# Spectral filter and MLP, two layers: the first quad's layer norm in the output stage, the middle's staging buffers, and three smaller placements

## The chip, the cores and the metric

The kernel runs on one NeuronCore of a Trainium2 chip. The metric is the device time of one execution, in microseconds. The engines that matter are TensorE (PE, matmuls; its weight loads are shown as PEld), VectorE (DVE), ScalarE (ACT), GpSimd (POOL) and SyncE (SP, here an issuer of DMAs). Each engine runs its own instructions in order, and they wait for each other through semaphores.

## The reference

An array x of 2048 rows (sequence) and 576 columns goes twice through a spectral layer and an MLP, each with a residual:

```
def _A_ref(x, w_r, w_i):                       # spectral
    X = rfft2(x); X = X * (w_r + 1j * w_i)
    return irfft2(X, s=(S, D))
def _B_ref(x, w1, b1, w2, b2):                 # MLP
    y = _layernorm(x)
    h = gelu(y @ w1 + b1)                      # 576 -> 4608
    return h @ w2 + b2                         # 4608 -> 576
x = x + _A_ref(_layernorm(x)); x = x + _B_ref(_layernorm(x))     # and once more
```

Inputs and the result are bf16.

## The kernel before

The 2048 rows stand in SBUF as 16 tiles of 128 rows (`x_sb`), and the tiles are worked in the order `order`, four quads of four tiles. The Fourier transforms are matmuls with constant matrices. Each of the two layers has these stages.

- **First transform** (`SpectralIn`): along the columns, then the first step along the rows, with an exchange through DMAs into `vx`. In layer 1 nearly all of it is done inside the MLP of layer 0.
- **Middle** (`middle`, L610): for each of 16 groups n, `dft_u` transforms on TensorE into a two-bank accumulator (`big_ps`, of which there are three) and ScalarE copies it to a staging buffer `xs` (L623). `weigh` multiplies it on VectorE with the filter's real and imaginary part (L632, L633), `join` adds or subtracts the products (L639, L641), `idft_c` (L654) transforms back into another of the three accumulators, ScalarE copies the result to `h` (L662), and a DMA exchanges it into `hx` (L602). The loop issues `dft_u(i)`, then `idft_c(i-4)`, then `weigh(i)`. The `xs` buffers are three, two in `shared` and one in `h_sb`.
- **Output stage** (`SpectralOut`, L682): `idft_v(n)` (L696) transforms rows into a small accumulator (`sm_ps`, one bank, of which there are two), ScalarE copies it to `u2` (L703). `idft_v_rest(q)` (L728) does the last 34 rows for four tiles at once and is copied to `u2r` (L733). `idft_k(n)` (L753) transforms along the columns into a two-bank accumulator, and `add(n)` puts the result on x with VectorE (L773 for both halves, then L781 and L782, which `add(n+1)` issues as the odd part of tile n). Four tiles (`early`) have x put into the accumulator by TensorE and take a copy on ScalarE (L765) and two adds (L767).
- **Layer norm of the first quad**, by `Prep`, inside the output stage: sums and squares on ScalarE (L833), the moments on VectorE (L842 to L844), the root on ScalarE (L848), reciprocal and shift on VectorE (L853, L854), then a norm for each of four tiles, on VectorE (L875) or ScalarE (L862), each with a copy of the last 64 columns (L878 on VectorE, L865 on GpSimd), and `turn` (L895): five transposes on TensorE into a small accumulator and a copy to `yT` (L897). `pieces[n]` and `behind_add[n]` in `run_all` (L784) say behind which tile each of these is issued.
- **MLP**: `mlp_up` (L919, L927, gelu L933) for a quad of four tiles, then `mlp_down` (L966) for each tile, 72 matmuls into one two-bank accumulator and one add (L989). The last tile of a layer runs its two column halves one after the other (L971 to L982); in the last layer each half has its own accumulator and is stored with its own DMA.

The program's order on TensorE, VectorE, ScalarE and GpSimd is the order in which the code issues it (`manual_schedule`, L240). SP's order is the scheduler's: it puts each DMA where its waits allow. A wait belongs to a whole tile: a tile is one buffer or accumulator, and a writer waits for its readers even where they use other parts of it. An accumulator that is asked for goes to the buffer that is free first, and its first writer waits for the last reader of what stood there.

Of the kernel before, what the change touches and what calls it, by code (L numbers as in the profile page):

```python
# [161 lines left out]
def kernel(  # L162
# [447 lines left out]
    def middle(vx, hx, wks, i1s, loads, ahead, steps):  # L610
        st = {}
        r_sb = shared_tile(BF16)

        def dft_u(n):
            e = E_ORDER[n]
            for call in steps.get(n, ()):
                call()
            px = ahead.px[n] if n in steps else big_ps([P, 2, 512])
            for o, terms in ((0, ((0, 0), (1, 1))), (1, ((0, 1), (2, 0)))) if n not in steps else ():
                for q, (pl, ri) in enumerate(terms):  # L620
                    nc.tensor.matmul(px[:, o, 0:KP], lhsT=c_f2[:, n // 4, pl, n % 4, :], rhs=vx[:, E_SLOTS.index(e), ri, :], start=(q == 0), stop=(q == 1))  # L621
            xs = at(r_sb, [P, 2, KP], 592 * (n % 3)) if n % 3 < 2 else at(h_sb, [P, 2, KP], 4 * GROUP + 2 * 592 + 1024)
            nc.scalar.copy(out=xs[:], in_=px[:, :, 0:KP])  # L623
            st["xs", n] = xs

        def weigh(n):
            wk = wks[n // 4]
            xs = st.pop(("xs", n))
            ma, mb = (at(r_sb, [P, 2, KP], 592 * (2 + 4 * b + n % 4)) for b in (0, 1))
            wr = wk[:, n % 4, 0:1, 0:KP].to_broadcast([P, 2, KP])  # L630
            wi = wk[:, n % 4, 1:2, 0:KP].to_broadcast([P, 2, KP])
            nc.vector.tensor_mul(out=ma[:], in0=xs[:], in1=wr)  # L632
            nc.vector.tensor_mul(out=mb[:], in0=xs[:], in1=wi)  # L633
            st["m", n] = ma, mb

        def join(n):
            ma, mb = st.pop(("m", n))
            xp = at(r_sb, [P, 2, KP], 592 * (2 + 8 + n % 3))
            marks["xp", n] = nc.vector.tensor_sub(out=xp[:, 0, :], in0=ma[:, 0, :], in1=mb[:, 1, :]).ins  # L639
            if n not in SUMS_ON_PE:  # L640
                marks["xp", n] = nc.vector.tensor_tensor(out=xp[:, 1, :], in0=ma[:, 1, :], in1=mb[:, 0, :], op=ALU.add).ins  # L641
            for call in loads.get(n, ()):
                call(("xp", n))
            st["xp", n] = xp[:, 0], (ma[:, 1], mb[:, 0]) if n in SUMS_ON_PE else (xp[:, 1],)

        def idft_c(n):
            re, im = st.pop(("xp", n))
            i1 = i1s[n // 4]
            ph = big_ps([P, 2, 512])
            odd = big_ps([P, 2, 512]) if n == NT - 1 else ph  # L650
            for o, (p_re, p_im) in enumerate(((0, 2), (1, 0))):
                terms = [(p_re, re)] + [(p_im, part) for part in im]
                for q, (pl, rhs) in enumerate(terms):
                    nc.tensor.matmul(  # L654
                        (ph, odd)[o][:, o, 0:KP], lhsT=i1[:, pl, n % 4, :], rhs=rhs, start=(q == 0), stop=(q == len(terms) - 1)
                    )
            h = at(r_sb, [P, 2, KP], 592 * (13 + n % 8)) if n % 8 < 6 else at(h_sb, [P, 2, KP], 4 * GROUP + 592 * (n % 8 - 6))
            if n == NT - 1:
                nc.scalar.copy(out=h[:, 0], in_=ph[:, 0, 0:KP])
                ins = nc.vector.tensor_copy(out=h[:, 1], in_=odd[:, 1, 0:KP]).ins  # L660
            else:
                ins = nc.scalar.copy(out=h[:], in_=ph[:, :, 0:KP]).ins  # L662
            marks["h", n] = ins
            exchange(hx, E_ORDER[n], h, nc.gpsimd if n < NT - 3 else nc.sync, N_FIRST if n == NT - 1 else 0)
            st["h"] = h

        for i in range(NT + 4):
            if i < NT:
                dft_u(i)
            if 0 <= i - 4 < NT:  # L670
                idft_c(i - 4)
            if NT < i < NT + 3:
                keep_busy(1)
            if i < NT:
                weigh(i)
            for n in (i,) if i < 3 else range(max(3, i - 1), min(i, NT)):
                join(n)
        return st["h"]
# [3 lines left out]
    class SpectralOut:  # L682
# [33 lines left out]

        def idft_v_rest(self, q):

            pr = sm_ps([P, 4, P], F32)
            for i in range(4):  # L720
                for part, p0 in ((0, 0), (1, 64)):
                    cs = slice(part * 128, part * 128 + 128)
                    n = 4 * q + i
                    terms = [(self.hx[:, n, ri], c_r1[:, ri, cs]) for ri in range(2)]
                    if n < N_FIRST:
                        terms += [(self.late_h[:, ri], r1_late[:, n, ri, cs]) for ri in range(2)]
                    for k, (rows, rhs) in enumerate(terms):
                        nc.tensor.matmul(  # L728
                            pr[p0 : p0 + 64, i, :], lhsT=rows[:, KP - 64 : KP], rhs=rhs, start=(k == 0), stop=(k == len(terms) - 1)
                        )  # L730
            u2r = u2r_buf[u2r_turn[0] % 2]
            u2r_turn[0] += 1
            nc.scalar.copy(out=u2r[:], in_=pr[:])  # L733
            self.st["u2r", q] = u2r
# [49 lines left out]
        def run_all(self, prep, loads):  # L784

            pieces = {n: [] for n in range(NT)}
            for n, (i, k) in zip((1, 2, 3, 4, 5, 5, 6, 7), ((i, k) for i in range(4) for k in range(2))):
                pieces[n].append(lambda i=i, k=k: prep.sum(i, k))
            pieces[10].append(prep.root)
            for i, m in enumerate((13, 14, 14)):  # L790
                pieces[m].append(lambda i=i: prep.turn(i, "act"))
            behind_add = {9: [prep.moments], 11: [prep.scale_sums, lambda: prep.norm(0, nc.vector)], 12: [lambda: prep.norm(2, nc.vector)]}
            pieces[12].append(lambda: prep.norm_act(1))
            pieces[13].append(lambda: prep.norm_act(3))
            for n in self.early[:2]:
                self.put_x(n)
            for n in range(N_FIRST):
                self.idft_v_late(n)
            keep_busy(7, big_ps)
            self.idft_v(0)  # L800
            for call in loads:
                tc.add_manual_dep(call(), marks["u2", 0].name, SYNC, reason="pace of the loads")
            self.idft_v(1)
            self.idft_v_rest(0)
            self.idft_v(2)
            for n in range(NT):
                if n == NT - 1:
                    prep.turn(3, "act")
                if n in self.early[2:]:
                    self.put_x(n)  # L810
                self.idft_k(n)
                self.add(n)
                for call in behind_add.get(n, ()):
                    call()
                if 0 < n < NT - 2:
                    self.idft_v(n + 2)
                if n % 4 == 1 and n + 3 < NT:
                    self.idft_v_rest(n // 4 + 1)
                for call in pieces[n]:
                    call()  # L820
            self.add(NT)

    class Prep:
# [35 lines left out]
        def norm_act(self, i):  # L859
            rs, shift = self.rs_shift  # L860
            xn = work.tile([P, 640], BF16, tag="xn", bufs=3)
            nc.scalar.activation(  # L862
                out=xn[:, 0:D], in_=x_sb[:, self.quad[i], :], func=ACT.Identity, bias=shift[:, i : i + 1], scale=rs[:, i : i + 1]
            )
            nc.gpsimd.tensor_copy(out=xn[:, D:640], in_=xn[:, D - 64 : D])  # L865
            self.st[i] = xn
# [90 lines left out]
    def mlp_down(t, i, hts, store, between):  # L957
# [2 lines left out]
        xr = x_sb[:, t, :].rearrange("p (h n) -> p h n", h=2)  # L960
        nc.vector.tensor_tensor(out=xb[:], in0=xr, in1=b2_bc[:].rearrange("p (h n) -> p h n", h=2), op=ALU.add)  # L961
        po = big_ps([P, 2, 512])
        parts = [po, big_ps([P, 2, 512]) if t == order[-1] and store else po]

        def step(fc, h):
            nc.tensor.matmul(  # L966
                parts[h][:, h, 0:DH], lhsT=hts[fc][:, i * 128 : (i + 1) * 128], rhs=w2_chunk(fc)[:, h * DH : (h + 1) * DH],
                start=(fc == 0), stop=(fc == NFC - 1),
            )

        if t == order[-1]:  # L971
            for n in range(2 * NFC):
                h, fc = divmod(n, NFC)
                step(fc, h)
                if fc == NFC - 1:
                    nc.vector.tensor_tensor(out=xr[:, h], in0=parts[h][:, h, 0:DH], in1=xb[:, h], op=ALU.add)
                    if store:
                        nc.sync.dma_start(out=ov[:, t, h * DH : (h + 1) * DH], in_=xr[:, h])
                if n % 12 == 11:
# [13 lines left out]
    def mlp(li, prep, spec, loads):  # L993
# [3 lines left out]
        for q in range(4):  # L997
# [6 lines left out]
                spec.ahead = Ahead(spec.vx, spec.st)  # L1004
            for i, t in enumerate(QUADS[q]):
                if q == 3 and spec is not None and i == 2:
                    for out, in_ in ((spec.ahead.w[96:128], late_ap), (c_k1_late[:], k1_late_ap[1])):
                        ins = nc.sync.dma_start(out=out, in_=in_).ins
                        tc.add_manual_dep(ins, marks["ht", NFC - 1].name, SYNC, reason="pace of the loads")
                slots = {k: [] for k in range(6)}  # L1010
                if q < 3 and i == 0:
                    slots[0].append(prep.stats)
# [135 lines left out]
```

## Time and profile before

| | us |
|---|---|
| median of three runs (730.92, 732.32, 732.39) | 732.32 |
| the profiled execution | 730.92 |
| its span | 729.2 |

TensorE's granted clock is 1.0 throughout. Busy time and number of instructions by stage, from the windows of the profile (us from the span's start):

| stretch | what | PE | DVE | ACT | POOL |
|---|---|---|---|---|---|
| 32.0 to 58.9 | layer 0, end of the first transform and middle | 25.44 | 20.83 | 18.73 | 7.77 |
| 58.9 to 85.0 | layer 0, output stage | 24.74 | 19.90 | 21.69 | 1.95 |
| 85.0 to 387.0 | layer 0, MLP, with layer 1's first transform | 301.62 | 113.74 | 111.71 | 27.81 |
| 387.0 to 414.4 | layer 1, end of the first transform and middle | 26.70 | 19.52 | 19.68 | 14.43 |
| 414.4 to 440.4 | layer 1, output stage | 24.57 | 19.77 | 21.56 | 0.48 |
| 440.4 to 729.2 | layer 1, MLP and the last store | 285.40 | 46.21 | 88.93 | 13.45 |

How to read it: TensorE is busy nearly all the time. In the MLPs the other engines have more than half of the time to spare; in the middle and the output stage, two times 27 and 26 us, all three compute engines are busy for three quarters of the time or more. A line of the timeline gives the start, the time from the first start to the last end, engine, source line, operation, what is written from what, and in brackets the idle time before it with what ended it. A line of the chain gives start, length and what was on the path.

### The profile page before, as it was taken

What the parts mean: (1) busy time and instruction counts of PE and PEld (TensorE: products, weight loads), DVE (VectorE), ACT (ScalarE), POOL (GpSimd) and SP (SyncE); (2) the same over time, 40 slices, a digit from 0 to 9 for tenths busy, and PEclk for the clock granted to TensorE, in tenths of its full rate; (3) what the DMA queues carried; (4) which work ended last, traced back from release to release, by engine and by line L of the source; (5) the groups of instructions that cost most, each with busy time, mean ns of one, the idle gap of its engine ahead of it and who ended that gap; (6) DMA issues with size and microseconds to landing.
All of it is one profiled execution on the core that took longest, in us unless ns stands there. A gap on an engine that the chain in (4) does not pass through costs nothing.

```text
span 729.2 us, 12472 instructions
## 1 busy us (share of the span) xinstructions
PE 718.1 (98%) x5078; PEld 456.9 (63%) x5078; DVE 267.0 (37%) x917; ACT 309.5 (42%) x534; POOL 79.5 (11%) x139
## 2 busy tenths in 40 slices
PE   8999999999999999999999999999999999999998
PEld 5777645864587448744877674477447744774476
DVE  7894910664055504520367586011400140110011
ACT  7796764026411651156216686610550056005600
POOL 4240112002000200000006301200100010000000
PEclk9999999999999999999999999999999999999999
DMA  9788345211111111100217402530102010200000
GB/s 291 215 194 202 141 150 194 66 44 54 37 39 50 55 32 41 47 7 1 59 40 235 134 2 71 188 115 18 44 1 45 17 45 1 45 19 8 1 17 17
DMA packets 52722, 54.33 MB, mean 75 GB/s; under 512 B 31576, under 2 KB 43624, under 8 KB 52664
## 3 DMA queue, kind: packets, MB, share of 16 engines
q1 hardware_dynamic: 43784, 25.99, 13.5%
q0 software_dynamic: 8448, 26.96, 11.7%
q8 instruction: 40, 0.66, 0.4%
q10 hardware_dynamic: 432, 0.58, 0.2%
q14 instruction: 18, 0.15, 0.1%
HBM read 29.31 MB, written 8.59 MB: 52 GB/s over the span
## 4 chain that ended last, share of the span: by engine, by line
PE 95%; ACT 2%; DVE 1%; DMA 1%; issue 0%; SPq 0%; POOL 0%; ACTq 0%; POOLq 0%
PE psb_4486 L966 1%; PE psb_6902 L966 1%; PE psb_6304 L966 1%; PE psb_5706 L966 1%; PE psb_4228 L966 1%; PE psb_4100 L966 1%; PE psb_3294 L966 1%; PE psb_2492 L966 1%; PE psb_2126 L966 1%; PE psb_1998 L966 1%; PE psb_7654 L966 1%; PE psb_7577 L966 1%; PE psb_7500 L966 1%; PE psb_7185 L966 1%; PE psb_7108 L966 1%; PE psb_6587 L966 1%
## 5 line engine op out<-in xcount | busy, mean ns | idle before, releaser
L966 PEld LDWEIGHTS <-h_sb 128*128 128x128 bf16 x2304 | 224.9, 98 | 57.8 <-issue 0.2
L919 PEld LDWEIGHTS <-w_sb 128*128 128x128 bf16 x1152 | 109.5, 98 | 142.4 <-issue 17.2
L875 DVE TENSOR_SCALAR xn<-x_sb,mv,rs 128x576 bf16<-128x576 bf16 x24 | 9.4, 427 | 67.2 <-DMA quad_1818<-xn 28.9
L333 DVE BATCH_NORM_STATS2 stats<-x_sb 128x6 f32<-128x288 bf16 x78 | 30.8, 437 | 0.0
L927 PEld LDWEIGHTS <-w1r_sb 64*128 64x128 bf16 x288 | 10.8, 94 | 24.5 <-issue 17.0
L961 DVE TENSOR_TENSOR xb<-x_sb,b_bc 128x576 f32<-128x576 bf16 x32 | 24.0, 749 | 0.0
L878 POOL COPY xn<-xn 128x64 bf16<-128x64 bf16 x24 | 6.4, 268 | 150.7 <-DVE xn L875 150.7
L654 PEld LDWEIGHTS <-h_sb 128*128 128x128 bf16 x160 | 15.4, 97 | 5.5 <-DVE shared_721 L639 0.6
L933 ACT ACTIVATE h_sb<-psb_6064,b_sb 128x512 bf16<-128x512 f32 x2 | 1.3, 684 | 37.9 <-PE psb_6064 L927 37.9
L933 ACT ACTIVATE h_sb<-psb_7260,b_sb 128x512 bf16<-128x512 f32 x2 | 1.3, 684 | 37.8 <-PE psb_7260 L927 37.8
L933 ACT ACTIVATE h_sb<-psb_6662,b_sb 128x512 bf16<-128x512 f32 x2 | 1.3, 684 | 37.8 <-PE psb_6662 L927 37.8
L989 DVE TENSOR_TENSOR x_sb<-psb_7500,xb 128x576 bf16<-128x576 f32 x1 | 0.8, 758 | 43.4 <-PE psb_7500 L966 43.4
L989 DVE TENSOR_TENSOR x_sb<-psb_4100,xb 128x576 bf16<-128x576 f32 x1 | 0.8, 758 | 39.5 <-PE psb_4100 L966 39.5
L415 DVE TENSOR_TENSOR xf<-ef 128x256 bf16<-128x256 f32 (+1 forms) x56 | 13.6, 305 | 0.5
L621 PEld LDWEIGHTS <-c_f_84 128*128 128x128 bf16 x108 | 10.4, 97 | 4.4 <-DMA v_sb<-w_sb 1.1
L989 DVE TENSOR_TENSOR x_sb<-psb_6902,xb 128x576 bf16<-128x576 f32 x1 | 0.8, 757 | 33.6 <-PE psb_6902 L966 33.6
L989 DVE TENSOR_TENSOR x_sb<-psb_6304,xb 128x576 bf16<-128x576 f32 x1 | 0.8, 758 | 33.6 <-PE psb_6304 L966 33.6
L502 PEld LDWEIGHTS <-c_k_82 128*128 128x128 bf16 x112 | 10.4, 98 | 2.3
L989 DVE TENSOR_TENSOR x_sb<-psb_3294,xb 128x576 bf16<-128x576 f32 x1 | 0.8, 759 | 28.7 <-PE psb_3294 L966 28.7
L989 DVE TENSOR_TENSOR x_sb<-psb_2492,xb 128x576 bf16<-128x576 f32 x1 | 0.8, 758 | 28.7 <-PE psb_2492 L966 28.7
L833 ACT ACTIVATE h_sb<-x_sb 128x576 bf16<-128x576 bf16 x16 | 11.2, 700 | 0.1
L486 PEld LDWEIGHTS <-xT 128*128 128x128 bf16 x96 | 9.3, 97 | 3.1 <-issue 0.7
(1422 smaller groups left out, 1534.5 us busy)
## 6 DMA issues: line engine op xcount, KB each, us to landing
w_sb<-in_B_w_dram SPq DMA_DIRECT2D x16, 288.0 KB
v_sb<-in_B_w_dram POOLq DMA_DIRECT2D x4, 1152.0 KB, 6.5
shared_1512<-in_B_w_dram POOLq DMA_DIRECT2D x2, 1440.0 KB, 7.5
shared_5461<-in_B_w_dram POOLq DMA_DIRECT2D x2, 1440.0 KB, 7.6
out_dram<-x_sb SPq DMA_DIRECT2D x15, 144.0 KB
v_sb<-w_sb POOLq DMA_DIRECT2D x13, 145.0 KB, 4.9
x_sb<-in_A_x_dram SPq DMA_DIRECT2D x3, 576.0 KB
b_sb<-shared_721 POOLq DMA_DIRECT2D x11, 145.0 KB, 4.8
```

The lines of the kernel that those rows point to most:

```text
L333: nc.vector.bn_stats(out=stats[:, h, :], in_=x_sb[:, t, h * DH : (h + 1) * DH])
L415: nc.vector.tensor_tensor(out=xf[:, at0 : at0 + 2 * n].rearrange("p (g d) -> p g d", g=2), in0=ef[:, :, first : first + n], in1=ef[:, :, b ...
L486: nc.tensor.matmul(pz[:, o, 0:KP], lhsT=xT[:, ci, :], rhs=c_fd[:, 3 * o + q, :], start=(q == 0), stop=(q == 2),)
L502: nc.tensor.matmul(py[:, r, 0:KP], lhsT=(c_k1_late if t in LATE else c_k1)[:, pl, :], rhs=z[:, ri], start=(q == 0), stop=(q == 1))
L621: nc.tensor.matmul(px[:, o, 0:KP], lhsT=c_f2[:, n // 4, pl, n % 4, :], rhs=vx[:, E_SLOTS.index(e), ri, :], start=(q == 0), stop=(q == 1))
L654: nc.tensor.matmul((ph, odd)[o][:, o, 0:KP], lhsT=i1[:, pl, n % 4, :], rhs=rhs, start=(q == 0), stop=(q == len(terms) - 1))
L833: nc.scalar.activation(out=at(h_sb, [P, D], 512 * 34), in_=x_sb[:, self.quad[i], :], func=(ACT.Copy, ACT.Square)[k], accum_out=self.s12[:, ...
L875: nc.vector.tensor_scalar(out=xn[:, 0:D], in0=x_sb[:, self.quad[i], :], scalar1=mean, scalar2=rs, op0=ALU.subtract, op1=ALU.mult)
L919: nc.tensor.matmul(acc[p][q], lhsT=w1_sb[:, ci, fc * 128 : (fc + 1) * 128], rhs=yT[:, ci, :], start=(first and ci == 0), stop=(not first a ...
L927: nc.tensor.matmul(acc[p][q], lhsT=w1r_sb[rows, p, :], rhs=yT[rows, 4, :], start=first, stop=not first)
L961: nc.vector.tensor_tensor(out=xb[:], in0=xr, in1=b2_bc[:].rearrange("p (h n) -> p h n", h=2), op=ALU.add)
L966: nc.tensor.matmul(parts[h][:, h, 0:DH], lhsT=hts[fc][:, i * 128 : (i + 1) * 128], rhs=w2_chunk(fc)[:, h * DH : (h + 1) * DH], start=(fc = ...
```

## The change

Five edits, and a function that one of them needs:

1. `dft_u`: the `xs` buffers are two, both in `shared`, instead of three.
2. `idft_v_rest(0)`, the first 34-row transform of the output stage, takes one of the three two-bank accumulators instead of one of the two small ones.
3. The first quad's layer norm. Moments behind `add(8)` instead of `add(9)`, the root behind tile 8 instead of 10, reciprocal and shift and norm 0 behind `add(9)` instead of `add(11)`. Norm 1 goes to GpSimd (new `norm_pool`), behind `add(9)`; norm 2 goes from VectorE to ScalarE, behind tile 10; norm 3 is on ScalarE behind tile 12 instead of 13. The turns are issued behind tiles 11, 12, 13 and 14 in the order 0, 2, 1, 3, instead of behind 13, 14, 14 and ahead of 15 in the order 0 to 3.
4. The last MLP tile of the last layer has both halves in one two-bank accumulator, as the last tile of layer 0 has.
5. The two late loads of layer 0's last quad no longer wait for the last gelu.
6. `norm_pool`, the new function, is `norm` with its arithmetic on GpSimd.

In the built instruction order, the load of `c_k1_late` for layer 1 stands on SP's queue much earlier: behind layer 0's last exchange of the first transform and ahead of the loads of the middle. GpSimd's queue holds one more instruction, a library reload, between the last exchange of layer 0's middle and the first norm.

```diff
-            xs = at(r_sb, [P, 2, KP], 592 * (n % 3)) if n % 3 < 2 else at(h_sb, [P, 2, KP], 4 * GROUP + 2 * 592 + 1024)
+            xs = at(r_sb, [P, 2, KP], 592 * (n % 2))
...
-            pr = sm_ps([P, 4, P], F32)
+            pr = (sm_ps if q else big_ps)([P, 4, P], F32)
...
-            pieces[10].append(prep.root)
-            for i, m in enumerate((13, 14, 14)):
-                pieces[m].append(lambda i=i: prep.turn(i, "act"))
-            behind_add = {9: [prep.moments], 11: [prep.scale_sums, lambda: prep.norm(0, nc.vector)], 12: [lambda: prep.norm(2, nc.vector)]}
-            pieces[12].append(lambda: prep.norm_act(1))
-            pieces[13].append(lambda: prep.norm_act(3))
+            behind_add = {8: [prep.moments], 9: [prep.scale_sums, lambda: prep.norm(0, nc.vector), lambda: prep.norm_pool(1)]}
+            pieces[8].append(prep.root)
+            pieces[10].append(lambda: prep.norm_act(2))
+            pieces[12].append(lambda: prep.norm_act(3))
+            for n, i in ((11, 0), (12, 2), (13, 1), (14, 3)):
+                pieces[n].append(lambda i=i: prep.turn(i, "act"))
...
-                if n == NT - 1:
-                    prep.turn(3, "act")
...
+        def norm_pool(self, i):
+            mean, rs = self.mr[i]
+            xn = work.tile([P, 640], BF16, tag="xn", bufs=3)
+            nc.gpsimd.tensor_scalar(
+                out=xn[:, 0:D], in0=x_sb[:, self.quad[i], :], scalar1=mean, scalar2=rs, op0=ALU.subtract, op1=ALU.mult
+            )
+            nc.gpsimd.tensor_copy(out=xn[:, D:640], in_=xn[:, D - 64 : D])
+            self.st[i] = xn
...
-        parts = [po, big_ps([P, 2, 512]) if t == order[-1] and store else po]
...
-                parts[h][:, h, 0:DH], lhsT=hts[fc][:, i * 128 : (i + 1) * 128], rhs=w2_chunk(fc)[:, h * DH : (h + 1) * DH],
+                po[:, h, 0:DH], lhsT=hts[fc][:, i * 128 : (i + 1) * 128], rhs=w2_chunk(fc)[:, h * DH : (h + 1) * DH],
...
-                    for out, in_ in ((spec.ahead.w[96:128], late_ap), (c_k1_late[:], k1_late_ap[1])):
-                        ins = nc.sync.dma_start(out=out, in_=in_).ins
-                        tc.add_manual_dep(ins, marks["ht", NFC - 1].name, SYNC, reason="pace of the loads")
+                    nc.sync.dma_start(out=spec.ahead.w[96:128], in_=late_ap)
+                    nc.sync.dma_start(out=c_k1_late[:], in_=k1_late_ap[1])
```

More of the change, by code (lines that the diff above doesn't have):

```diff
@@ L975, in mlp_down @@
                 if fc == NFC - 1:
-                    nc.vector.tensor_tensor(out=xr[:, h], in0=parts[h][:, h, 0:DH], in1=xb[:, h], op=ALU.add)
+                    nc.vector.tensor_tensor(out=xr[:, h], in0=po[:, h, 0:DH], in1=xb[:, h], op=ALU.add)
                     if store:
```

## The prediction

> **What bounds the kernel now.** I read the page's first lines and its chain of work first, for the time and the engine on the path.
>
> ```profile
> span 729.2 us, 12472 instructions
> PE 95%; ACT 2%; DVE 1%; DMA 1%; issue 0%; SPq 0%; POOL 0%; ACTq 0%; POOLq 0%
> ```
>
> TensorE is on the path for 95% of the span; only places where it is held up can give or cost time. The profiled execution took 730.92 us (1.7 around its span), the lowest of three; the median, 732.32, is 1.4 above. I sum against 730.92 and add 1.4.
>
> The chain in order of time, at the end of the first layer's output stage:
>
> ```profile
> 80.92 0.29 PE pss_1459 L895 x5
> ...
> 81.56 0.70 ACT yT_1408 L897
> 82.26 0.77 ACT xn L862
> 83.02 1.81 ACT yT_1408 L897 x3
> 84.83 0.04 issue
> 84.88 1.89 PE psb_1514 L919 x8
> ```
>
> TensorE has 4 turns (0.29) and 2 row transforms (0.73) left at 80.92, 2.62 us; the MLP begins 3.96 later. So 1.34 us are lost per layer (the second layer shows it at 438.55 to 440.41), to ScalarE's norms and turns. That is what the change aims at. The timeline of the same place shows who is just behind:
>
> ```profile
> 79.84 0.59 ACT L703 CAST u_1437<-pss_1432 128x512 bf16<-128x512 f32 x1 [0.59 <-PE pss_1432 L696]
> 80.32 0.87 ACT L862 ACTIVATE xn<-x_sb,shift,rs 128x576 bf16<-128x576 bf16 x1
> 83.17 0.75 DVE L773 TENSOR_TENSOR shared_1047<-psb_1469,x_sb 128x576 f32<-128x576 f32 x1
> 84.20 0.45 DVE L782 TENSOR_TENSOR x_sb<-shared_1047,psb_1442 128x288 bf16<-128x288 f32 x1
> ```
>
> The last line ends at 84.65 and frees tile 13's accumulator, which the MLP's first pair takes. VectorE is thus only 0.18 behind ScalarE's 84.83.
>
> The middle (L610), where a third xs buffer goes, in the timeline:
>
> ```profile
> 38.98 0.66 ACT L623 CAST shared_721<-psb_779 128x580 bf16<-128x580 f32 x1
> 39.52 0.67 ACT L662 CAST shared_721<-psb_785 128x580 bf16<-128x580 f32 x1
> 39.58 0.45 DVE L633 TENSOR_TENSOR shared_721<-h_sb 128x580 bf16<-128x580 bf16 x1
> 39.69 0.66 PE L654 MATMUL psb_803<-shared_721,h_sb 128*128 128x290 bf16 x4
> 42.36 0.91 PE L654 MATMUL psb_841<-shared_721,h_sb 128*128 128x290 bf16 x6 [0.32 <-DVE shared_721 L639]
> ```
>
> ScalarE copies tile 4 (38.98) before VectorE has weighed tile 2 (L633, to 40.03). From 42.36 the chain is TensorE without a break to the stage's end, so what is late there stays late.
>
> Last, the chain at both layers' last MLP tile, the first of which keeps both halves in one accumulator already:
>
> ```profile
> 378.12 1.48 PE psb_4486 L966 x12
> 379.61 0.02 issue
> 379.63 0.47 DVE x_sb L976
> 380.10 0.04 issue
> 380.14 4.58 PE psb_4486 L966 x36
> ...
> 716.99 4.41 PE psb_7731 L966 x36
> 721.39 4.42 PE psb_7732 L966 x36
> ```
>
> With one accumulator the second half waits for VectorE's read of the first; with two it doesn't.
>
> **The change, part by part.**
>
> *Last tile, one accumulator:* from the first half's end to the second's took 5.12 us in layer 0 (379.61 to 384.73) against 4.42. **+0.70**. Nothing is behind it but the last add and store, which move along.
>
> *Two xs buffers.* The copy of tile n now waits for the second product (L633) of tile n-2. Layer 0: tile 2's ends at 40.03, so tile 4's copy starts at 40.06, not 38.98. Behind it on ScalarE: h of tile 0 (39.52) goes to 40.60 (copies start 0.54 apart) and ends 41.27; tile 5's copy, held by tile 3's product until 41.34, runs 41.37 to 42.02. TensorE has three accumulators, so idft_c(1) (psb_803) waits for tile 4's copy: 40.06 + 0.64 + 0.05 = 40.75, not 39.69; idft_c(2) waits for tile 5's copy, 42.06; tile 6's copy comes after h of tile 1 (from 41.91) at 42.46 and ends 43.11, so idft_c(3) (psb_841) starts at 43.15, not 42.36. **+0.79**. In layer 1 tile 2's product ends at 394.45: tile 4's copy 394.47 (was 394.29), tile 5's 395.77 (held by the product that ends 395.74), h of tile 1 396.31, tile 6's copy 396.86 to 397.54, idft_c(3) 397.59, not 397.18. **+0.41**. Later copies find their product done, since TensorE then sets the pace. Bounds: 0 if these waits are soaked up, and +1.1 a layer if the largest one seen (39.69 to 40.75) stays; I take the chain's values.
>
> *Output stage, VectorE.* The moments (three starts, 76.29 to 76.84, 0.55) go behind tile 8's add; reciprocal, shift and norm 0 (78.97 to 79.80, 0.83) behind tile 9's; norm 2 with its 64-column copy (81.19 to 81.78, **0.59**) leaves VectorE. Tile 9's odd adds then end at about 78.40 rather than 77.57 and free the accumulator of tile 12 then; that transform now starts after turn 0, at 78.87, which hides it (cost without: 0.1). The root comes after the new var (about 75.45) and holds back u of tile 11 from 75.16 to 75.75; its reader starts at 77.24.
>
> *Turns and ScalarE.* Norms 2 and 3 stay on ScalarE, at 10 and 12. TensorE from the end of idft_v(13) at 78.58: turn 0 to 78.87, tile 12 to 79.60, idft_v(14) to 80.04, turn 2 to 80.33, tile 13 to 81.06, idft_v(15) to 81.50, then turn 1. But the small accumulators are two: turn 1 takes turn 2's. ScalarE: u of 14 at 80.13, norm 3 at 80.61 (0.48 later, as 79.84 to 80.32), turn 2's copy at 81.38 (0.77 later), ended 82.08. Turn 1 runs 82.12 to 82.41, **0.62 of new wait**; tile 14 to 83.14, turn 3 to 83.43, tile 15 to 84.16. ScalarE's last copy ends at 84.19, but VectorE's add of tile 14 starts at 83.17, just where it stood before, and with it tile 13's odd adds end at 84.65. The MLP starts at about 84.78 instead of 84.88: the 0.59 that VectorE saved goes into waiting for tile 14. **-0.1** a layer. Bounds: -0.65 (turn 1 doesn't wait, VectorE's 84.06 decides) to +0.3 (copies 0.1 slower each).
>
> *Norm 1 on GpSimd.* The trace has no such row. From below, its memsets (1740 columns 1.55, 1160 in 1.07, 0.83 ns a column): 0.5 us for 576. From above, its 64-column copy (0.25) nine times: 2.25. I take 1.3, between. It starts at about 77.1; its result is first wanted by turn 1, but norm 2's 64-column copy stands behind it on GpSimd and is wanted by turn 2 at 80.04. With two copies of 0.25 the cover is 2.4 us: nothing, and about 1 us a layer per us above. Behind it on GpSimd are the memset L1110 and w2 loads that wait for a gelu at 89.84.
>
> In the built instruction order a library reload stands on GpSimd's queue, before the first of these norms and after the last exchange; GpSimd stood idle for 26.5 us there (to 81.23), so I price it at nothing, between 0 and the 1.28 of the nearest row, ScalarE's table load (L933), and either is covered. [...]
>
> *First 34-row transform in a two-bank accumulator.* It no longer waits for u_1080 (0.24 us before 60.26), so u2r ends at 61.52, not 61.76. But tile 0's transform takes the same accumulator back and starts at 61.56: its third matmul, which wanted u2r at 61.81 before, comes at 61.80. **0**, between -0.24 and +0.1.
>
> *Late loads without their wait.* c_k1_late moves up SP's queue to between the last exchange (issued by 34.75) and the load at 38.01, where SP is idle; 0.4 us of issue, hidden, 0.4 without. The other stays behind its memset. Between 0 and +0.4.
>
> Sum: 0.70 + 0.79 + 0.41 - 0.2 = **+1.7**: 732.6 as the profiled execution, **734.0** on the median.
>
> **The rivals.**
> *Not slower:* turn 1 doesn't wait, because ScalarE is through turn 2's copy by 81.5, 0.6 sooner than I have it. Then the MLP starts on VectorE's 84.06: -0.65 a layer, sum +0.6, 732.9. For it: GpSimd takes work off, and only 0.6 us of order decides. Against it: norm 3 stands ahead of that copy.
> *GpSimd late:* decides beyond 2.4 us. At 4.5, twice the upper bound, norm 2's copy ends at 82.1, turn 2 runs to 82.44, tile 13 to 83.17, idft_v(15) to 83.61, turn 1 to 83.90, tile 14 to 84.63; VectorE's add of it and tile 13's odd adds take 1.48 more (83.17 to 84.65) and the MLP starts at 86.25, 1.4 late, in both layers: 0.70 + 0.79 + 0.41 + 2.8 = +4.7, 737.0. For it: no such row. Against it: the 2.25.
> *Faster:* the whole 1.34 comes out of both layers and the middle loses little, sum about -2, 730.3. The same turn order speaks against it.
>
> **How the numbers follow.** What this kernel's measurement can tell from no change is 0.2%, 1.46 us, so 1.7 lies just above. Forecast 0.56 (0.04 of it, below 1.46, within 0.2%), GpSimd late 0.10: slower 0.62. Not slower 0.28, so within 0.2% 0.32. Faster 0.06. The forecast's own range is 733.2 (less one layer's 0.55 at the turns and 0.24 at the first 34-row transform) to 735.0 (the middle's 1.1 in both layers). I take 732.1 to 736.0: below the not-slower case by half of the 1.47 that the three runs span, and most of the way to late GpSimd.
>
> **What would show it.** In the profile after: tile 4's copy (L623) released by VectorE, and idft_c(3) 0.8 and 0.4 later against the stage's start; turn 1 released by ScalarE's copy of turn 2; tile 14's first add of VectorE idle before it, waiting for TensorE; the last tile's second half released by VectorE, 0.70 later. It would be wrong if the middle's tail took up the 0.79, or if turn 1 followed idft_v(15) at once.

## The result, and the profile after

| | before | after |
|---|---|---|
| median of six runs each, us | 731.62 | 733.46 (733.05 to 734.26) |
| ratio, with its 95% interval | | 1.0026 (1.0014 to 1.0039) |
| the profiled execution | 730.92 | 733.05 |
| its span | 729.2 | 731.3 |

The change makes the kernel 1.84 us slower (1.0 to 2.9 by the interval). The forecast was +1.7 with 734.0, in a range of 732.1 to 736.0. Three more runs moved the median of the kernel before to 731.62, 0.70 below the 732.32 from which 734.0 was counted; counted from the new one the forecast is 733.3. The page of the changed kernel, its first line and the shares of the chain by engine:

```profile
span 731.3 us, 12478 instructions
...
PE 93%; ACT 3%; DVE 2%; DMA 1%; issue 1%; ACTq 0%; DVEq 0%
```

TensorE's share of the chain is down from 95%, those of ScalarE and VectorE are up by one point each: more of the path runs through them.

Where the time went is read from the profile after, whose source lines stand a few lines off from those of before (L975 to L982, L895 to L902 and so on). The first view is the chain of work of the changed kernel at the end of layer 0's output stage: start, length, what was on the path.

```profile
78.53 0.60 DVE xn L885
79.14 0.36 DVE x_sb L781
79.50 0.37 DVE x_sb L782
79.87 0.04 issue
79.91 0.90 PE psb_1432 L753 x6
...
81.33 0.59 ACT u_1447 L703
81.92 0.77 ACT xn L860
82.69 0.59 ACT yT_1352 L904
83.28 0.04 issue
83.32 0.44 PE pss_1476 L902 x5
...
86.16 1.89 PE psb_1514 L926 x8
```

It reads from top to bottom as two waits of TensorE. At 79.91 tile 12's transform waits for VectorE's odd adds of tile 9, which stand behind a 64-column copy (L885) that took 0.60. At 83.32 turn 1 waits for ScalarE's copy of turn 2, which stands behind norm 3 (81.92). The MLP's first matmul is at 86.16, against 84.88 before. The timeline of the same place adds idle times:

```profile
78.14 2.44 POOL L869 TENSOR_SCALAR xn<-x_sb,mean,rs 128x576 bf16<-128x576 bf16 x1 [22.34 <-DVE rs L851]
81.08 0.44 PE L902 MATMUL pss_1452<-ident,xn 128*128 128x128 bf16 x5
83.32 0.44 PE L902 MATMUL pss_1476<-ident,xn 128*128 128x128 bf16 x5 [0.63 <-ACT yT_1352 L904]
84.53 0.76 DVE L773 TENSOR_TENSOR shared_1047<-psb_1483,x_sb 128x576 f32<-128x576 f32 x1 [0.49 <-PE psb_1483 L753]
```

GpSimd's norm takes 2.44 us. With the two 64-column copies behind it GpSimd is done at 81.05, and turn 2, which wants the second of them, starts at 81.08. Turn 1 waits 0.63, and VectorE then stands idle for 0.49 until tile 14 is there.

The middle of layer 0, in the timeline:

```profile
40.34 0.64 ACT L623 CAST shared_721<-psb_779 128x580 bf16<-128x580 f32 x1 [0.66 <-DVE shared_721 L633]
41.04 0.66 PE L654 MATMUL psb_803<-shared_721,h_sb 128*128 128x290 bf16 x4 [0.65 <-ACT shared_721 L623]
43.44 0.90 PE L654 MATMUL psb_841<-shared_721,h_sb 128*128 128x290 bf16 x6
```

Tile 4's copy is now held by VectorE's second product (L633) of tile 2, and TensorE, short of an accumulator, by that copy. `idft_c(3)` (psb_841) starts 1.08 later than before, of which 0.20 was there before the middle began. At the stage's end 0.74 is left (26.49 against 25.75 in the table below). And the last tile, in the chain:

```profile
718.40 4.42 PE psb_7731 L972 x36
722.82 0.02 issue
722.85 0.47 DVE x_sb L982
...
723.36 4.58 PE psb_7731 L972 x36
...
727.96 0.46 DVE x_sb L982
```

The second half waits for VectorE's read of the first, as it does in layer 0; from one half's add to the other's 5.11 us pass instead of 4.41.

### The profile page after: what moved, and what is told of

It reads as the page before. It is cut to its first block, busy times and chain, and to the rows that moved or that the text cites. A ratio compares the mean times of both kernels' runs of the same rounds, so it can differ in the third digit from the quotient of the medians.

```text
span 731.3 us, 12478 instructions
## 1 busy us (share of the span) xinstructions
PE 719.6 (98%) x5078; PEld 457.1 (63%) x5078; DVE 267.4 (37%) x913; ACT 309.4 (42%) x534; POOL 84.6 (12%) x143
## 4 chain that ended last, share of the span: by engine, by line
PE 93%; ACT 3%; DVE 2%; DMA 1%; issue 1%; ACTq 0%; DVEq 0%
PE psb_4486 L972 1%; PE psb_7731 L972 1%; PE psb_2800 L972 1%; PE psb_1998 L972 1%; PE psb_7500 L972 1%; PE psb_6902 L972 1%; PE psb_6304 L972 1%; PE psb_4358 L972 1%; PE psb_3602 L972 1%; PE psb_3294 L972 1%; PE psb_2671 L972 1%; PE psb_2492 L972 1%; PE psb_1759 L972 1%; PE psb_7654 L972 1%; PE psb_7577 L972 1%; PE psb_7185 L972 1%
## 5 line engine op out<-in xcount | busy, mean ns | idle before, releaser
L885 POOL COPY xn<-xn 128x64 bf16<-128x64 bf16 x24 | 6.4, 267 | 150.7 <-DVE xn L882 150.7
```

## The experiments

Twelve kernels were run. All were timed against the kernel before on the same chip. The table has each one's median against that, and five stages taken from the start times in its profile's timeline: the middles from the first matmul of L579 (the part of `dft_u` that is done ahead of the loop) to `idft_v(0)`, the output stages from there to the MLP's first matmul, and the tail from the last tile's first add to its second.

| kernel | against before, us | ratio (95%) | middle 0 | output 0 | middle 1 | output 1 | tail |
|---|---|---|---|---|---|---|---|
| before | | | 25.75 | 25.89 | 26.79 | 25.89 | 4.41 |
| after | +1.84 | 1.0026 (1.0014 to 1.0039) | 26.49 | 26.23 | 26.80 | 25.98 | 5.11 |
| e1_halves | +1.17 | 1.0019 (1.0010 to 1.0028) | 26.63 | 26.14 | 28.13 | 25.97 | 4.41 |
| e2_xs3 | +0.86 | 1.0010 (1.0001 to 1.0019) | 25.67 | 26.14 | 26.43 | 25.96 | 5.12 |
| e3_order | +0.81 | 1.0010 (1.0002 to 1.0019) | 26.60 | 25.57 | 27.72 | 25.38 | 5.12 |
| e4_out | +0.22 | 1.0000 (0.9991 to 1.0009) | 25.73 | 26.14 | 26.55 | 25.97 | 4.41 |
| e5_norm_vec | +1.75 | 1.0028 (1.0018 to 1.0038) | 26.50 | 26.14 | 27.60 | 25.98 | 5.12 |
| e6_twice | +6.47 | 1.0091 (1.0077 to 1.0104) | 26.52 | 28.69 | 27.18 | 28.60 | 5.12 |
| e7_best | -1.03 | 0.9988 (0.9979 to 0.9996) | 26.00 | 25.58 | 26.01 | 25.40 | 4.41 |
| e9_best_vec | -0.76 | 0.9991 (0.9982 to 0.9999) | 26.32 | 25.50 | 26.21 | 25.40 | 4.41 |
| e8_rest | +1.82 | 1.0026 (1.0014 to 1.0037) | 26.54 | 26.21 | 27.52 | 26.03 | 5.12 |
| e10_copy | -0.41 | 0.9997 (0.9988 to 1.0006) | 26.06 | 25.82 | 27.00 | 25.57 | 4.41 |
| e12_copies | -1.20 | 0.9987 (0.9978 to 0.9996) | 25.76 | 25.48 | 26.88 | 25.39 | 4.41 |
| e13_xs2 | +1.37 | 1.0020 (1.0011 to 1.0029) | 26.64 | 26.10 | 27.54 | 25.88 | 4.41 |

The stages come from one profiled execution each. Those that the edits leave alike repeat to 0.1 us, but for the first output stage of e13_xs2 (0.21 above that of the kernel before) and for the middles, where transfers from buffer to buffer land at different times (layer 1's last exchange in 3.64 to 4.63 us). The medians are over 4 to 11 runs, with intervals of 0.6 to 1 us to either side. Where the two disagree by some tenths, both reasons are possible, and the runs don't part them.

**e1_halves: the tail alone undone.**

```diff
+        parts = [po, big_ps([P, 2, 512]) if t == order[-1] and store else po]
-                po[:, h, 0:DH], lhsT=hts[fc]...
+                parts[h][:, h, 0:DH], lhsT=hts[fc]...
-                    nc.vector.tensor_tensor(out=xr[:, h], in0=po[:, h, 0:DH], ...
+                    nc.vector.tensor_tensor(out=xr[:, h], in0=parts[h][:, h, 0:DH], ...
```

> The changed kernel with the last tile's two halves in separate accumulators again, as before. My theory: the tail alone comes back, 0.70 us: the second half (L972's line) follows the first at once, and its last add ends 0.7 sooner against the first half's start, which stays 1.4 late. Against the kernel before +1.1 instead of +1.84. Rival: the two-bank accumulator of the separate half costs elsewhere (it takes one from the tile before), then less than 0.4 comes back.

The tail is 4.41 again, so the whole 0.70 comes back in that stage, against the rival's 0.4; the kernel is at +1.17 instead of +1.84, 0.67 less. The theory holds.

**e2_xs3: the third xs buffer alone given back.**

```diff
-            xs = at(r_sb, [P, 2, KP], 592 * (n % 2))
+            xs = at(r_sb, [P, 2, KP], 592 * (n % 3)) if n % 3 < 2 else at(h_sb, [P, 2, KP], 4 * GROUP + 2 * 592 + 1024)
```

> The changed kernel with three xs buffers in the middle again. My theory: in layer 0 tile 4's copy (L623) is no longer held, idft_c(3) starts 0.8 to 1.0 sooner against the stage's start and v(0) with it, so 0.8 comes back. In layer 1 idft_c(3) comes 0.5 sooner, but the changed kernel's profile has the last exchange landing 0.4 faster there (3.72 against 4.12 us); if that transfer's time is chance, 0.4 to 0.5 comes back in layer 1 as well (-1.3 in all, +0.5 against before); if the late middle itself makes the transfer short, 0 does (-0.8, +1.0 against before), and the transfer takes 4.1 again. Rival: the middle isn't what is late; then v(0) in layer 0 stays where it is.

Middle 0 falls from 26.49 to 25.67. The whole comes to +0.86, so 0.98 came back, between the two cases named. The transfer took 3.96 us here, and 3.64 to 4.63 over all profiles, with a median of 3.72 in the seven with two buffers and of 4.01 in the seven with three. Whether the late middle makes it shorter isn't settled: of those seven, four had another late transfer (see e13_xs2), and the other three took 3.72, 4.09 and 4.63.

**e3_order: turn 2 ahead of norm 3.**

```diff
-            pieces[12].append(lambda: prep.norm_act(3))
             for n, i in ((11, 0), (12, 2), (13, 1), (14, 3)):
                 pieces[n].append(lambda i=i: prep.turn(i, "act"))
+            pieces[12].append(lambda: prep.norm_act(3))
```

> The changed kernel with one pair swapped on ScalarE: turn 2 and its copy go ahead of norm 3 behind tile 12. My theory: turn 1's wait of 0.63 us (for turn 2's copy, which stands behind the norm's 0.87) is the step that sets the MLP's start, so without it turn 1 follows at once, VectorE's add of tile 14 starts 0.5 sooner (VectorE itself is free 0.48 sooner) and the MLP 0.5 sooner in each layer: -1.0 in all, +0.8 against before. Rival: norm 3 is now 0.77 later, turn 3 waits for it and for u of tile 15, and the MLP for turn 3's copy: 0 to -0.2 a layer.

+0.81, and 0.66 and 0.60 less in the two output stages than in the changed kernel's profile. From the timeline of e3_order:

```profile
81.71 0.70 ACT L904 COPY yT<-pss 128x640 bf16<-128x640 bf16 x1
82.46 0.44 PE L902 MATMUL pss<-ident,xn 128*128 128x128 bf16 x5
85.47 2.75 PE L926 MATMUL psb<-yT,w_sb 128*128 128x512 bf16 x11 [0.59 <-DVE x_sb L782]
```

The copy of turn 2 starts 0.49 after u of tile 14 (81.22), turn 1 at 82.46 follows `idft_v(15)` (81.98) without a wait, and the MLP is released by VectorE's odd adds. This is the "not slower" rival of the prediction, made to happen.

**e4_out: the output stage's edits alone** (e1_halves and e2_xs3 together).

> The changed kernel with separate halves and three xs buffers, so that only the output stage's edits (and the two late loads' pace) are left. My theory: the output stage costs 0.33 us in layer 0 and 0.16 in layer 1 as the two profiles show it from tile 11 to the MLP's first matmul, so +0.5 against before, against my prediction's -0.2. Rival: the loss in the output stage is an effect of the late start that the middle hands on (other DMA timing), and then it is within 0.1 of before in each layer.

The stages are +0.25 and +0.08 against before, less than the 0.33 and 0.16 of the theory; in layer 1 it is as little as the rival allows, in layer 0 it isn't, though the middle is as before. The whole is +0.22, which the measurement can't tell from nothing, and less than half of the +0.5 expected.

**e5_norm_vec: norm 1 back on VectorE.**

```diff
-            behind_add = {8: [prep.moments], 9: [..., lambda: prep.norm_pool(1)]}
+            behind_add = {8: [prep.moments], 9: [..., lambda: prep.norm(1)]}
```

> The changed kernel with norm 1 on VectorE, behind norm 0, in place of GpSimd. The output stage is read from v(0) to the MLP's first matmul: 26.23 and 25.98 us in the changed kernel's two layers, 25.89 before. Theory A: the 2.44 us on GpSimd buys nothing, since VectorE's 64-column copy beside it takes 0.60 instead of 0.18; with norm 1 back, VectorE has 0.43 more and the copy takes 0.18 again, tile 9's odd adds end within 0.15 of where they were, and the stage keeps its time within 0.15 in each layer, the whole within 0.3. Rival B: GpSimd's work beside VectorE is itself the cost of the stage (tile 12's transform waits 0.26 for those odd adds); then -0.25 a layer. Rival C: GpSimd's help is worth the whole instruction, 0.43 to 0.6 a layer, and the time goes up by about 1.

Theory A: +1.75, and the stages keep their time (26.14 and 25.98). From its timeline:

```profile
78.67 0.18 DVE L885 COPY xn<-xn 128x64 bf16<-128x64 bf16 x1
78.77 0.42 DVE L882 TENSOR_SCALAR xn<-x_sb,mean,rs 128x576 bf16<-128x576 bf16 x1
```

Without GpSimd's norm beside it the copy takes 0.18, and from its start to the end of norm 1 pass 0.52 (78.67 to 79.19), less than the 0.60 that the copy alone took.

**e6_twice: GpSimd's norm written twice.**

```diff
+            nc.gpsimd.tensor_scalar(
+                out=xn[:, 0:D], in0=x_sb[:, self.quad[i], :], scalar1=mean, scalar2=rs, op0=ALU.subtract, op1=ALU.mult
+            )
             nc.gpsimd.tensor_scalar(
                 out=xn[:, 0:D], in0=x_sb[:, self.quad[i], :], scalar1=mean, scalar2=rs, op0=ALU.subtract, op1=ALU.mult
             )
```

> The changed kernel with GpSimd's norm 1 written twice (the same values into the same tile), so that it holds its queue for 4.88 us instead of 2.44. My theory: the cover is used up at 2.44 (norm 2's 64-column copy, queued behind it, ends at 81.05 and turn 2 starts at 81.08), so that copy ends at 83.50, turn 2 runs at 83.54 instead of 81.08, turn 1 directly behind v(15) at about 85.0, VectorE's add of tile 14 at 86.2 instead of 84.53 and the MLP starts 1.6 to 1.7 later in each layer: +3.3 in all, +5.1 against before. Rival: the cover is wider (turn 1's wait of 0.63 and VectorE's queue decide, not norm 2's copy): under +0.8 a layer.

The cover is used up, as the theory says: the part of turn 2 that wants the late copy waits 2.03 us. But the whole is +6.47, 1.4 more than expected, and the output stages grow by 2.46 and 2.62 instead of 1.6 to 1.7. Its table of stretches shows what the expectation lacked (after the stretch: busy time and number of PE, PEld, DVE, ACT and POOL, then the granted clock of TensorE and the DMA share):

```profile
82.00:84.00 2.00, 0.78 (x7) 0.66 (x8) 0.37 (x2) 0.93 (x2) 1.53 (x5) 1.00 0.01 4
84.00:86.00 2.00, 2.00 (x16) 1.53 (x14) 1.48 (x3) 1.35 (x3) 1.29 (x1) 0.60 0.02 4
86.00:88.00 2.00, 2.00 (x13) 1.50 (x12) 1.30 (x3) 0.75 (x2) 0.00 (x0) 0.54 0.00 0
```

After the stall TensorE runs at half clock: in half-microsecond stretches the grant is 0.91 at 84.0, 0.50 from 84.5 to 87.5 and 1.00 again from 88.0. That is about 3.4 us at half clock (0.09, 3.0 and, at 0.67 to 88.0, 0.33), in which TensorE does 1.7 us less than at the full one (in the chain a tile's transform takes 0.73 at 83.45 and 1.44 at 85.22). In layer 0 the chain is TensorE without a break from 83.22 to 88.30, so its clock sets the time there. About half of the 1.7 shows, 0.8 to 0.9 a layer over the expectation; by the expectation's sum TensorE would at full clock have waited for VectorE in part of that time. The changed kernel shows 1.00 through the same place.

**e7_best and e9_best_vec: the output stage with the better order, and before's middle and tail** (e4_out with e3_order's swap; e9_best_vec also has e5_norm_vec's edit).

> The output stage's edits with turn 2 ahead of norm 3, and with before's separate halves and three xs buffers. From the stages of the runs so far: output stage 25.57 and 25.38 us against before's 25.89, middle and tail as before: -0.8 against before, 730.6. Rival: the two exchanges whose landing varies by 1 us and more from run to run hide it, or the middle takes the gain: within 0.3 of before.

> As e7_best, and norm 1 on VectorE instead of GpSimd. With turn 1's wait gone VectorE is what the MLP waits for (tile 13's odd adds), so VectorE's load counts now: by theory A of e5_norm_vec the stage stays within 0.15 a layer of e7_best's; by rival B it is 0.25 a layer faster; by rival C it is 0.4 to 0.6 a layer slower than e7_best, and the whole 0.1 to 0.4 above before.

e7_best is 1.03 us faster than before (0.3 to 1.5 by the interval), with the stages at 25.58 and 25.40. Its middle 0 (26.00) waited for a load of constants (`h_sb<-const_i`) that landed 9.07 us after its issue; e9_best_vec and e10_copy show the same wait (9.36 and 9.06). e9_best_vec has the same stages (25.50 and 25.40), so where VectorE is the bound, too, GpSimd's norm buys nothing: theory A again.

**e8_rest: the first 34-row transform and the two late loads as before.**

```diff
-            pr = (sm_ps if q else big_ps)([P, 4, P], F32)
+            pr = sm_ps([P, 4, P], F32)
-                    nc.sync.dma_start(out=spec.ahead.w[96:128], in_=late_ap)
-                    nc.sync.dma_start(out=c_k1_late[:], in_=k1_late_ap[1])
+                    for out, in_ in ((spec.ahead.w[96:128], late_ap), (c_k1_late[:], k1_late_ap[1])):
+                        ins = nc.sync.dma_start(out=out, in_=in_).ins
+                        tc.add_manual_dep(ins, marks["ht", NFC - 1].name, SYNC, reason="pace of the loads")
```

> The changed kernel with the first 34-row transform in the small accumulator again and the two late loads waiting for the last gelu again, as before: both edits that my prediction put at nothing. My theory: the same within 0.3 us of the changed kernel (733.3 to 733.6 against a before of 731.5), v(0) to tile 0's transform in layer 0 2.5 to 2.6 us. Rival: the small accumulator's wait (0.24 in the kernel before) comes back on the path in each layer, +0.5; or the loads' earlier start had cost 0.4 in layer 0's middle or at layer 1's start, -0.4.

+1.82 against the +1.84 with these two edits, and the stages without a late transfer agree with the changed kernel's to 0.05: no cost or gain of either shows.

**e10_copy and e12_copies: the copy beside GpSimd's norm taken off VectorE.** e10_copy is e7_best with

```diff
-            behind_add = {..., 9: [prep.scale_sums, lambda: prep.norm(0, nc.vector), ...]}
+            behind_add = {..., 9: [prep.scale_sums, lambda: prep.norm(0), ...]}
```

and e12_copies is e10_copy with norm 2's 64-column copy by `nc.scalar.copy`.

> e7_best with norm 0's 64-column copy on GpSimd, ahead of norm 1, instead of on VectorE beside it (where it takes 0.60). My theory: in e7_best VectorE's odd adds of tile 13 release the MLP (0.59) and nothing else is within 0.5 us of it (the last turn's copy ends 84.37, tile 15's transform 84.39, the MLP starts 84.98), so VectorE's 0.52 goes straight into the time: output stage 25.58 to about 25.05 in layer 0, 25.40 to 24.9 in layer 1, and the whole about -2 against before. Norm 2's copy on GpSimd ends 0.24 later, against a last part of turn 2 that would want it 0.2 sooner; that may give back up to 0.3 a layer. Rival: the copy beside GpSimd isn't what VectorE is late by; then within 0.2 of e7_best in all.

> e10_copy with norm 2's 64-column copy on ScalarE, which stands idle for 0.47 us behind the copy of turn 0, so that nothing wanted by turn 2 is queued behind GpSimd's norm. My theory: if norm 2's copy holds turn 2 in e10_copy, the rest of the gain comes here (up to 0.3 a layer more); if it doesn't, 0. Rival: the copy makes ScalarE late (u of tile 14, turn 0's copy) by its 0.2 a layer.

The expectation of e10_copy fell: its stages are 0.24 and 0.17 longer than e7_best's, not 0.5 shorter. VectorE was freed and tile 12's transform came at once, but norm 2's copy on GpSimd now ends at 81.00, the last fifth of turn 2 waits for it (0.45), and VectorE then waits 0.69 for tile 13:

```profile
81.05 0.23 PE L902 MATMUL pss<-ident,xn 128*128 128x128 bf16 x1 [0.45 <-POOL xn L863]
82.05 0.76 DVE L773 TENSOR_TENSOR shared<-psb,x_sb 128x576 f32<-128x576 f32 x1 [0.69 <-PE psb L753]
```

In e12_copies that wait is gone and the stage is 25.48 and 25.39, only 0.10 and 0.01 below e7_best: VectorE still idles 0.35 before tile 13's add, since `idft_v(14)` now waits for u of tile 13 to free a small accumulator (79.69) and turn 2 for the copy of turn 0 (80.29). Three limits, VectorE, the small accumulators and GpSimd's queue, lie within half a microsecond of each other here. At -1.20 e12_copies is the fastest kernel run, though not to be told from e7_best.

**e13_xs2: the two xs buffers alone**, in the kernel before (the line of e2_xs3 the other way round).

> The kernel before with two xs buffers and nothing else of the change. My theory: in layer 0 the middle takes 0.8 longer (26.5 to 26.6 us from its first late-plane matmul to v(0), against 25.7 to 25.8 undisturbed), in layer 1 the last exchange is issued 0.4 to 0.5 later (22.95 us from the same point, against 22.3 to 22.5), and the whole is +1.2 to +1.3 (from the profiles so far), with the output stage at 25.89 and the tail at 4.41 as before. Rival: in layer 1 the transfer of y lands late only with two buffers (it held the middle in three of the profiles with two and in none of those with three); then about a further 1 us on average, and this profile is likely to show the wait for it.

Middle 0 is 26.64 and the whole +1.37, a little above the theory. The profile shows the rival's wait, too; the chain in layer 1:

```profile
390.64 4.59 DMA b_sb<-y
395.23 0.14 issue
395.36 1.15 PE psb L621 x8
```

The transfer of the last y takes 4.59 us and tiles of the middle wait 1.34 for it. It was on the chain in four of the seven profiles with two buffers (4.59 to 5.23 us) and in none of the seven with three. But it is issued before the first `xs` copy of the stage, and the order of the loads beside it is the same in both; what ties it to the buffers, if anything does, wasn't found. And since +1.37 is the median of 11 runs, it can't cost a microsecond in most of them. This stays open.

## Why the prediction was right, and where it was off

**Tail, +0.70:** right. 0.70 or 0.71 in every profile with one accumulator, 0.67 (e1_halves against after) and 0.64 (e4_out against e2_xs3) in the medians.

**Middle, +0.79 and +0.41:** right in the mechanism, with layer 1 probably put too low. `idft_c(3)` starts 0.88 and 0.50 later against the stage's start. Layer 0: 26.49 to 26.64 with two buffers in seven profiles, 25.67 to 25.76 with three where no load was late. Layer 1, measured to the issue of the last exchange, ahead of the transfers that vary: 22.95 in the changed kernel against 22.54 before, which is the 0.41; but over the profiles without a late y it is 22.94 to 22.97 against 22.18 to 22.54, whose mean is 22.36, and that makes 0.6. The medians give 0.98 (e2_xs3), 0.95 (e1_halves against e4_out) and 1.37 (e13_xs2) for both layers, to either side of the 1.20. What the prediction left out is the transfers behind it. The last exchange took 3.72 instead of 4.12 in the changed kernel's profile and gave layer 1's 0.41 back there; in the profiles with a late y it is among the fastest (3.64 to 3.74). Why isn't shown: in e3_order it was issued as late as in the changed kernel and took 4.63.

**Output stage, -0.1 a layer:** the step that was mis-sized. The mechanism is as predicted: turn 1's wait was put at 0.62 and is 0.63, VectorE's gain goes into waiting for tile 14, and the swap in e3_order, which takes the wait away, brought about 0.6 a layer, against 0.65 by the rival's sum. But the stage is +0.34 and +0.09 in the profile, +0.25 and +0.08 in e4_out. Tile 14's add was put at 83.17 in the time of before, which is 84.12 with the 0.95 that the stage was late already behind `idft_v(13)` (79.36 against 78.41); it came at 84.53. Of these 0.41, some 0.08 come from tile 12's wait for tile 9's odd adds. The prediction had these end at 78.40 and hid them behind turn 0; with the copy at 0.60 they ended at 79.87, 0.5 later than that in the same count, and tile 12's transform waited 0.26, less the 0.17 by which turn 0 came sooner than I had put it. The rest is two handovers that I had started when TensorE goes on to its next work: ScalarE's copy of u of tile 14 starts 0.25 after turn 2 has begun (81.33 and 81.08), where I had given it 0.09, and VectorE's add of tile 14 starts 0.20 after turn 3 has (84.53 and 84.33), where I had given it 0.03. By the timeline's rows, whose ends of matmuls are modelled, the last matmul ends 0.16 and 0.17 after TensorE's next instruction starts (81.24 and 81.08, 84.50 and 84.33), and the reader starts 0.09 and 0.03 behind that end. (e13_xs2, with before's output stage, shows 26.10 in layer 0 instead of 25.89, with ScalarE's turns 0.2 later, and 25.88 in layer 1; so single profiles of layer 0 can be off by that much, and the +0.08 of layer 1 is the firmer figure of the two.)

**Norm 1 on GpSimd, 1.3 taken, 0.5 to 2.25 as bounds:** 2.44, above the upper bound. Nine 64-column copies were no upper bound. Without VectorE's norm 0 and copy beside it the norm took 2.28 to 2.29 (e10_copy, e12_copies, the second one of e6_twice), just above the 2.25; beside them 2.43 to 2.44. That it still cost nothing directly is by luck of the cover, put at 2.4 and used to 0.03 (81.05 against 81.08). "GpSimd late" therefore had the right point from which it decides, as e6_twice shows, and its price was too low: beyond what its sum gives, the stages lost 0.8 to 0.9, with the clock at half. What the prediction did not see is the other side: the copy on VectorE beside it, 0.60 instead of 0.18, takes back the norm that GpSimd took over (e5_norm_vec, e9_best_vec).

**Library reload, nothing:** right. Its instruction took 0.037 us at 55.8, and the first norm behind it, at 78.1, took 2.44 like the second, 2.43, at 433.9. In this trace 22.34 us of idle GpSimd lay between the reload and the first norm, which could have hidden a cost. In e10_copy and e12_copies nothing could: there the reload stands directly in front of the norm, behind a copy, at 78.14 and 77.98, and the norm starts 0.10 later and takes 2.28:

```profile
L869 POOLq MODIFY_POOL_CONFIG  x2: 11/11/11, 78.1 to 78.1; - x2
L869 POOL TENSOR_SCALAR xn<-x_sb,mean,rs x1: 2283/2283/2283, 78.2 to 78.2; 128x576 bf16<-128x576 bf16 x1
```

So these two show no cost of the reload beyond that 0.10 us.

**First 34-row transform and late loads, 0:** right, as far as e8_rest can tell.

The sum: by medians 0.67 for the tail, 0.95 for the middle and 0.22 for the output stage. That these make the measured 1.84 says nothing, since each is the difference of neighbours in one row of kernels (the changed one, e1_halves, e4_out, before). Against the forecast's 0.70, 1.20 and -0.2, the output stage is 0.42 worse and the middle 0.25 better, so that +1.7 comes within 0.14 is in part luck; and with e13_xs2's 1.37 for the middle there would be no such balance. The intervals don't decide between the two.

## What to carry to other kernels

Before an instruction moves to another engine, ask what then stands in front of what in that engine's queue: a copy of 0.7 us behind a norm of 0.9 cost 0.6 us a layer, and swapping the two gave it back. Work that was moved to GpSimd was not free here even though it was covered: it took a norm of 0.42 off VectorE, and the copy beside it went from 0.18 to 0.60; compare both engines' rows. And count a handover from TensorE to a reader each time that the path takes it: here the reader started 0.20 to 0.25 us behind the point where TensorE went on.

## What the runs showed of the hardware

- GpSimd took 2.44 us for a norm of 128x576 bf16 (L869 of the changed kernel) that VectorE did in 0.42 (e5_norm_vec; 5.8 times), and 2.28 to 2.29 where neither norm 0 nor a 64-column copy ran on VectorE at the same time (e10_copy, e12_copies, the second one of e6_twice).
- A 64-column bf16 copy on VectorE took 0.60 (layer 0) and 0.52 (layer 1) beside that norm in the changed kernel, and 0.18 without it (e5_norm_vec). In layer 0 of the changed kernel, e3_order, e6_twice and e7_best, and in layer 1 of the changed kernel and e6_twice, the copy ended 0.98 to 0.99 us after GpSimd's norm had begun, whether it had itself begun 0.39 (layer 0) or 0.46 (layer 1) after. It thus looks held to a fixed point within GpSimd's instruction; no run varies this further. It was not held for the whole of it: in the changed kernel's layer 0 the copy ended 1.45 us before GpSimd's norm did (79.13 and 80.58). What holds it isn't shown. VectorE's adds from PSUM beside the norm kept their 0.44 (L781 and L782 at 79.05 and 79.42).
- A stall of 2.03 us on TensorE, with 1.97 us of work in the four around it (80 to 84 in layer 0, 439 to 443 in layer 1), was followed by about 3.4 us at a granted clock of 0.50, in both layers of e6_twice; the waits of 0.63 and 0.62 in the changed kernel were not (1.00 from 76 to 94 and from 434 to 444). What sets the lower clock off, and what ends it, no run here shows.
- The same transfer between buffers landed at different times from one profile to the next: the last exchange of layer 1 in 3.64 to 4.63 us over 14 profiles. This is more than most of the edits are worth, so layer 1's middle was judged up to the issue of its last transfer, and the whole by medians.
